# Gated linear attention into an expert layer: early low parts by TensorE and ScalarE, the forward scan in the gates' own tile, and a new order

## The chip, the cores and the metric

The kernel runs on one core of a Trainium2 chip. Time is device microseconds (us) of one execution, median of three. The engines are TensorE (PE; PEld is its weight load), VectorE (DVE), ScalarE (ACT), GpSimd (POOL) and SyncE (SP), which here only issues DMAs. Each engine works off its own list of instructions in the order of the program and waits on semaphores for the others.

## The reference

Two layers in float32. The first is a recurrence over 768 steps for each of 4 x 8 heads, with a 48 x 48 state; the second is an expert layer over all 3072 tokens:

```python
f = 1.0 / (1.0 + np.exp(-f_logit))
for t in range(S):                       # S = 768, B = 4, H = 8, D = 48
    state = f[:, :, t, :, None] * state + np.einsum('bhd,bhe->bhde', k[:, :, t], v[:, :, t])
    y[:, :, t] = np.einsum('bhd,bhde->bhe', q[:, :, t], state)
x = y.transpose(0, 2, 1, 3).reshape(B * S, H * D)      # 3072 x 384
h = x @ w_in                                           # 384 x 2048
return (h * np.clip(h + 3.0, 0.0, 6.0) / 6.0) @ w_out  # 2048 x 384
```

## The kernel before

**Units.** The recurrence is cut into 24 units: 6 chunks of 128 steps for each of 4 batches, all 8 heads at once; unit i is batch i % 4 of chunk i // 4. In a unit the gates go through a sigmoid on ACT (`gate`), and one DVE scan runs backwards over them (`back`, L320): products of the gates to the end of the chunk. They multiply k (`kmul`). The product over the whole chunk, limited below (`rend`, L336), is kept in `ends` and inverted (L337), and a second scan runs forwards from the inverse (`fwd`, L340, out into the tile `suffix` again); that multiplies q (`qmul`). TensorE then transposes k (`tk`, L404), forms scores (`att`, L385), the state's increment (`kv`, L423), and the output from the old state (`qs`, L454) and from the masked scores (`av`, L471). DVE masks (`mask`, L392); ACT or DVE carry the state on (`carry0`, `carry1`); `decay` multiplies the state by the chunk's product.

**Split numbers.** The large products run in fp32r, a faster format of TensorE that keeps fewer bits than float32. So each operand is split: a high part rounded to fp32r, and a low part, which is what is left. A product is three fp32r products: high x high, high x low, low x high. A unit's output y becomes a high part in `xts` by ACT (`xh`, L490) and a low part by DVE (`xl`, L493: y minus the high part); two DMAs (`hole`, L498) then fill rows between the heads.

**Conversion of the weights.** The 16 slices of weights (one per f, 128 columns of `w_in` and 128 rows of `w_out`) arrive as int64-packed float64 bits and are converted: loaded (`ld`), two pieces made by ACT (`z`, `cy`), the exponent's offset removed in 16-bit arithmetic on DVE (`mid`, `lim`, `dif`, `top`: L240, L246, L252, L256), the high part rounded by ACT (`high`, L261), the low part subtracted by DVE (`low` for a whole slice, or `lowi` and `lowo` for its halves: L264). For f = 0 to 7 the unrounded `w_out` slice is kept for a while (`wd`, a DMA).

**Expert layer.** Six groups of 512 tokens, 16 slices each. Token `mm1.n` (L517) is the first product of slice n % 16 of group n // 16: 9 fp32r instructions into one PSUM bank. ACT and DVE make the gate (`relu`, L527; `g`, L531), ACT the high part (`gh`, L536), DVE the low part (`gl`, L540), and `mm2.n` (L557) adds 9 fp32r instructions into three banks. In group 0, before its inputs are all there, slices 0 to 4 run as two halves of 256 tokens (`mm1a`, `mm1b`, L575), and slices 0 to 7 multiply by `w_out` in plain float32 (`mm2a`, `mm2b`, L593; `mm2x`, L565), which needs no `gh`, `gl` or `lowo`.

**Order.** Nothing is scheduled at run time. The table ORDER lists some 1360 tokens such as `mm1.35.4` (step, number, PSUM banks), written out ahead of time; each emits its instructions, and each engine keeps that order. `warm.n` are n products of zeros that keep TensorE's clock up. ON_POOL names the steps that run on GpSimd instead of DVE. Rings of buffers (`qkf` 3, `v` 3, `tg` 4, `gg` 3; `raw` 2, `w` 2, `y` 1) decide how far a step may run ahead.

Of the kernel before, what the change touches and what calls it, by code (L numbers as in the profile page):

```python
# [12 lines left out]
I16 = mybir.dt.int16  # L13
AF = mybir.ActivationFunctionType
# [25 lines left out]
qmul.0 qmul.1 kmul.3 decay.4 qmul.5 kmul.6 decay.6 kmul.7 decay.7 qmul.9 qmul.10 decay.10 qmul.11 decay.11 qmul.12  # L40
decay.12 qmul.13 decay.13 decay.14 kmul.15 qmul.15 kmul.16 decay.16 kmul.17 qmul.17 decay.17 qmul.18 decay.18 qmul.19
decay.19 qmul.20 decay.20 qmul.21 kmul.22 qmul.22 kmul.23 qmul.23 lowi.1 lowi.2 lowo.3 lowi.4 lowi.5 lowo.5 lowo.7
""".split()
ORDER = """
load.0 loadq.0 loadv.0 loadv.1 load.1 loadq.1 loadv.2 gate.0 ld.0 loadq.2 back.0 ld.1 rend.0 kmul.0 warm.16 tk.0.4
fwd.0 ktok.0 gate.1 qmul.0 load.2 warm.1 kv.0.0 carry0.0 back.1 att.0.2 carry1.0 qs.0.0 loadq.3 mask.0 rend.1 warm.2
av.0 kmul.1 xh.0 loadv.3 fwd.1 warm.1 tk.1.4 ktok.1 cy.0 xl.0 qmul.1 warm.1 kv.1.2 hole.0 z.0 load.3 att.1.0 carry0.1
mid.0 carry1.1 mask.1 warm.1 qs.1.2 lim.0 av.1 loadq.4 dif.0 xh.1 loadv.4 top.0 z.1 xl.1 gate.2 hole.1 cy.1 back.2
wd.0 ld.2 high.0 mid.1 kmul.2 rend.2 warm.12 tk.2.4 lowi.0 gate.3 fwd.2 ktok.2 warm.2 kv.2.0 lim.1 load.4 qmul.2
carry0.2 dif.1 att.2.2 carry1.2 back.3 ld.3 qs.2.0 mm1a.0.4 loadq.5 mask.2 kmul.3 rend.3 relua.0 av.2 ga.0 fwd.3  # L50
tk.3.2 xh.2 loadv.5 mm2a.0 ktok.3 z.2 xl.2 load.5 qmul.3 kv.3.2 gate.4 hole.2 top.1 att.3.0 carry0.3 carry1.3 mask.3
cy.2 wd.1 qs.3.2 loadq.6 back.4 av.3 high.1 loadv.6 xh.3 mid.2 kmul.4 xl.3 lowi.1 tk.4.4 mm1a.1.0 rend.4 hole.3 ktok.4
lim.2 fwd.4 gate.5 kv.4.2 relua.1 z.3 dif.2 ga.1 decay.4 ld.4 load.6 mm2a.1 top.2 back.5 cy.3 wd.2 mm1b.0.4 high.2
mid.3 kmul.5 mm1b.1.1 relub.0 lim.3 gb.0 lowi.2 tk.5.0 rend.5 relub.1 mm2b.0 carry0.4 ktok.5 dif.3 decay.5 ld.5
# [94 lines left out]
def gla_moe(ctx: ExitStack, tc: tile.TileContext, fg, qk, v, w, outT):  # L149
# [23 lines left out]
    weight = const.tile([128, NF, 2, WN], F32R, name="weight")  # L173
    win, wout = weight[:, :, :, :KT * 128], weight[:, :, :, KT * 128:]


# [645 lines left out]
```

## Time and profile before

| what | value |
|---|---|
| median of 3 runs | 513.59 us (512.88 to 513.95) |
| the profiled execution's own time | 512.78 us |
| its span, first to last instruction | 511.1 us |
| PE busy | 490.8 us (96%), 4960 instructions |
| DVE busy | 302.1 us (59%), 496 instructions |
| ACT busy | 207.1 us (41%), 331 instructions |
| POOL busy | 50.6 us (10%), 59 instructions |
| last product ends | 505.4 us; the rest is the last output |

Busy shares are means over the whole span. The prediction cuts the span into stages, and reads for each which engine never waits. The four parts of a row of the timeline are its start, its length, the engine and the instruction; idle time ahead of it and its releaser stand in brackets. In a row of grouped instructions the last part is idle time before them.

### The profile page before, as it was taken

Reading aid. Unit: us, or ns where it says so; the run is one execution under the profiler, and the core shown is the slowest. Engines: PE = TensorE matmul, PEld = TensorE weight load, DVE = VectorE, ACT = ScalarE, POOL = GpSimd, SP = SyncE. Lnnn points to the kernel's source line nnn. Section 1 sums busy time; section 2 is a strip of 40 time slices with the busy share of each in tenths; the row PEclk is TensorE's granted clock in tenths of the full one; section 3 lists DMA queues with packets and bytes.
Section 4 is the critical chain, followed back from the end, with each engine's and each line's share of the span. In section 5 each row is a group of like instructions: output and inputs, shape, how many; then the busy total and the mean of one; then the engine's idle time right before and its main releaser. Section 6 shows DMA issues by size and latency. Waiting matters only on the chain.

```text
span 511.1 us, 11476 instructions
## 1 busy us (share of the span) xinstructions
PE 490.8 (96%) x4960; PEld 388.7 (76%) x4960; DVE 302.1 (59%) x496; ACT 207.1 (41%) x331; POOL 50.6 (10%) x59
## 2 busy tenths in 40 slices
PE   8779999999999999999999999999999999999995
PEld 4468966777788888878887788887888788788874
DVE  5799999998955683364465524787433342333331
ACT  3556656764432253342242424244323341333231
POOL 2022422000211010020021000204000000000000
PEclk9899999999999999999999999999999999999999
DMA  8886666821302230330112200713300000200002
GB/s 279 260 246 194 216 200 233 256 94 41 99 19 79 62 99 0 109 96 16 52 28 81 62 0 2 191 56 106 87 0 1 8 1 0 63 1 1 0 1 67
DMA packets 25705, 43.53 MB, mean 85 GB/s; under 512 B 2608, under 2 KB 18224, under 8 KB 25648
## 3 DMA queue, kind: packets, MB, share of 16 engines
q1 hardware_dynamic: 25648, 42.73, 27.9%
q8 instruction: 41, 0.67, 0.5%
q14 instruction: 16, 0.13, 0.1%
HBM read 34.07 MB, written 4.72 MB: 76 GB/s over the span
## 4 chain that ended last, share of the span: by engine, by line
PE 51%; DMA 1%; DVE 1%; ACT 1%; issue 0%; POOL 0%; ACTq 0%
PE o L557 22%; PE pair L517 12%; PE single L517 11%; PE pair L608 3%; PE pair L454 1%; PE pair L471 1%; DMA qkf<-qk 1%; ACT tg L527 1%; PE pair L385 1%; DVE tg L531 1%; PE pair L423 1%; DMA outT<-os 1%; PE single L404 0%; PE pair L404 0%; DVE os L618 0%
## 5 line engine op out<-in xcount | busy, mean ns | idle before, releaser
L557 PE MATMUL o<-gg,weight 128*128 128x512 f32 x744 | 183.9, 398 | 0.6 <-ACT gg L536 0.6
L557 PEld LDWEIGHTS o<-gg,weight 128*128 128x128 f32 x744 | 138.2, 188 | 34.3 <-ACT gg L536 1.2
L517 PE MATMUL single<-xts,weight 128*128 128x512 f32 x423 | 108.2, 400 | 0.5 <-DVE tg L531 0.4
L517 PE MATMUL pair<-xts,weight 128*128 128x512 f32 x396 | 99.5, 396 | 0.6 <-DVE state L445 0.6
L540 DVE TENSOR_TENSOR gg<-tg,gg 128x512 fp32r<-128x512 f32 x88 | 60.6, 692 | 58.0 <-ACT gg L536 57.8
L517 PEld LDWEIGHTS single<-xts,weight 128*128 128x128 f32 x423 | 78.1, 188 | 20.4 <-DVE tg L531 1.2
L536 ACT ACTIVATE gg<-tg 128x512 fp32r<-128x512 f32 x88 | 55.4, 631 | 81.6 <-DVE tg L531 49.1
L517 PEld LDWEIGHTS pair<-xts,weight 128*128 128x128 f32 x396 | 73.5, 188 | 17.9 <-DVE state L445 1.0
L531 DVE SCALAR_TENSOR_TENSOR tg<-tg,single 128x512 f32<-128x512 f32 x47 | 32.1, 683 | 50.5 <-ACT tg L527 50.4
L527 ACT ACTIVATE tg<-single,half 128x512 f32<-128x512 f32 x47 | 32.3, 687 | 65.6 <-PE single L517 63.5
L531 DVE SCALAR_TENSOR_TENSOR tg<-tg,pair 128x512 f32<-128x512 f32 x44 | 30.0, 683 | 34.5 <-ACT tg L527 30.3
L527 ACT ACTIVATE tg<-pair,half 128x512 f32<-128x512 f32 x44 | 30.1, 687 | 35.3 <-PE pair L517 30.8
L490 ACT ACTIVATE xts<-pair 112x512 fp32r<-112x512 f32 x24 | 14.3, 595 | 53.8 <-PE pair L423 38.9
L320 DVE TENSOR_TENSOR_SCAN suffix<-gates,unit 112x516 f32<-112x516 f32 x24 | 30.2, 1261 | 6.7 <-ACT gates L314 6.4
L392 DVE TENSOR_TENSOR a<-pair,causal 128x512 f32<-128x512 f32 x24 | 16.4, 683 | 28.3 <-PE pair L471 26.1
L340 DVE TENSOR_TENSOR_SCAN suffix<-gates,rend 112x516 f32<-112x516 f32 x24 | 30.5, 1273 | 0.4 <-POOL qkf L333 0.2
L346 POOL TENSOR_TENSOR qkf<-qkf,suffix 112x512 f32<-112x512 f32 x16 | 21.5, 1345 | 88.1 <-DVE suffix L340 84.0
L349 POOL TENSOR_TENSOR decayed<-state,ends 112x192 f32<-112x192 f32 x13 | 7.0, 540 | 156.0 <-PE pair L454 123.5
L314 ACT ACTIVATE gates<-gates 112x512 f32<-112x512 f32 x24 | 15.0, 626 | 13.7 <-DMA gates<-fg 13.5
L493 DVE TENSOR_TENSOR xts<-pair,xts 112x512 fp32r<-112x512 f32 x24 | 16.4, 683 | 3.3 <-ACT xts L490 3.2
L385 PE MATMUL pair<-qkf 48*64 48x64 f32 x768 | 16.0, 220 | 2.4 <-issue 1.3
L423 PE MATMUL pair<-v,ktok 64*48 64x48 f32 (+1 forms) x768 | 15.9, 213 | 1.8 <-ACT ktok L411 1.0
(79 smaller groups left out, 420.7 us busy)
## 6 DMA issues: line engine op xcount, KB each, us to landing
raw<-w SPq DMA_DIRECT2D x16, 768.0 KB, 4.5
qkf<-qk SPq DMA_DIRECT2D x24, 448.0 KB, 4.4
gates<-fg SPq DMA_DIRECT2D x24, 226.2 KB, 3.0
v<-v SPq DMA_DIRECT2D x24, 200.0 KB, 4.3
outT<-os SPq DMA_DIRECT2D x17, 256.0 KB, 2.9
xts<-xts SPq DMA_DIRECT2D x48, 48.0 KB, 2.7
weight<-w SPq DMA_DIRECT2D x8, 192.0 KB, 3.3
outT<-os SPq DMA_DIRECT2D x2, 128.0 KB, 3.4
```

Source lines behind the costliest of these rows:

```text
L320: nc.vector.tensor_tensor_scan(flat(sf)[:, ::-1], gt[:, 1:][:, ::-1], flat(unit)[:, ::-1], 0.0, op0=ALU.mult, op1=ALU.add,)
L340: nc.vector.tensor_tensor_scan(flat(sf), gt[:, :NP * (C + 1)], flat(rend), 0.0, op0=ALU.mult, op1=ALU.add,)
L346: engine("qmul", i).tensor_tensor(parts_of(t, 0), parts_of(t, 0), split(sf[:, :, 1:]), op=ALU.mult)
L385: nc.tensor.matmul(d["at"][HC * odd:HC * (odd + 1), e, 2 * n + c], t[rs, 1, n, c, odd], t[rs, 0, n, c, odd], start=True, stop=True,)
L392: nc.vector.tensor_tensor(d["a"].rearrange("r p e t -> r e p t"), d["at"], causal.unsqueeze(1).unsqueeze(1).broadcast_to([128, 2, NP, HC]) ...
L423: nc.tensor.matmul(d["kv"][r:r + m, odd, c, n], d["ktok"][rs, 2 * n + part, r:r + m], heads_of(vt[rs], part, n, e)[:, :D], start=(odd, e) ...
L517: nc.tensor.matmul(h, win[:, f, a, k * 128:(k + 1) * 128], g["xt"][:, k, :g["n"] // C, b], start=i == 0, stop=i == 3 * KT - 1,)
L527: nc.scalar.activation(d["t"], d["h"], AF.Relu, bias=half, scale=1.0 / 6.0)
L531: nc.vector.scalar_tensor_tensor(d["t"], d["t"], 1.0, d["h"], op0=ALU.min, op1=ALU.mult)
L536: nc.scalar.activation(d["gg"][:, 0], d["t"], AF.Copy)
L540: engine("gl", f if g["name"] == "0" else NU).tensor_tensor(d["gg"][:, 1], d["t"], d["gg"][:, 0].bitcast(F32), op=ALU.subtract)
L557: nc.tensor.matmul(g["o"][m], wout[:, f, a, m * 128:(m + 1) * 128], g[f]["gg"][:, b], start=f == 0 and i == 0, stop=f == NF - 1 and i == 2 ...
```

## The change

Five things change, and the order of everything with them.

1. *Low parts of units 0 to 7.* A new constant, `minus`, is the negative of the identity, made by ACT at the start. A new step `ym` multiplies it with the high part of y and adds the product to y's PSUM bank, so that what is left there is the low part; `xl` is then a copy by ACT. Units 8 to 23 keep DVE's subtraction.
2. *Ends.* The limit from below (L336 before) is gone: the inverse is taken of the scan's own value, and ACT copies the value to `ends` (a new step `end`).
3. *Forward scan.* Its output overwrites the gates' tile instead of `suffix`. So `suffix` is free after `kmul`, `rend` and `end`, and the gates' tile is held until `qmul`.
4. *Conversion.* The 16-bit steps work on unsigned numbers with an offset; `lim` runs on ACT for f = 2, 4, 6, 8, 10, 12, 14 (ON_ACT) and ahead of `mid`. There are more tiles: `w` 3, `y` 2, and an own tile for `mid`, which before overwrote part of `raw`.
5. *Fewer float32 products.* Only slices 0, 1 and 2 run as halves with a float32 second product; slices 3 to 7 are full fp32r products. `wd`, `lowi` and `lowo` are there for f = 0, 1, 2 only; the rest uses `low`.

To make room, `tg` has 3 tiles and `gg` 2; the output's copies go through the `raw` ring; the last group keeps `gg` in tiles of `xts`. `warm` falls from 36 products to 27. ON_POOL is another list: 12 `kmul`, 13 `qmul`, 12 `decay`, `lowo.1`, `low.6`, `low.11`, `gl.9` (before 8, 16, 13, 4 `lowi` and 3 `lowo`).

```diff
+    minus = const.tile([PR, PR], F32R, name="minus")
+    nc.scalar.activation(minus, ident[:PR, :PR], AF.Copy, scale=-1.0)
...
-        {"qkf": 3, "v": 3, "ktok": 2, "tg": 4, "gg": 3, "a": 1},
+        {"qkf": 3, "v": 3, "ktok": 2, "tg": 3, "gg": 2, "a": 1},
...
-    cv = Ring(ctx.enter_context(tc.tile_pool(name="cv", bufs=1)), {"raw": 2, "w": 2, "y": 1})
+    cv = Ring(ctx.enter_context(tc.tile_pool(name="cv", bufs=1)), {"raw": 2, "w": 3, "y": 2, "t": 1})
...
     def conv_limit(f):
         y = conv[f]["y"]
-        nc.vector.tensor_scalar(
-            y, y, float(TOP_ONE - 32768), float(TOP_LAST), op0=ALU.max, op1=ALU.min
-        )
+        if on_scalar(f):
+            nc.scalar.activation(y, y, AF.Relu, bias=span, scale=-1.0)
+        else:
+            nc.vector.tensor_single_scalar(y, y, float(SPAN), op=ALU.min)
...
         def turn():
-            nc.vector.tensor_scalar_max(ends[:, i], sf[:, :, 0], END_LIMIT)
-            nc.vector.reciprocal(rend[:, :, 0], ends[:, i])
+            nc.vector.reciprocal(rend[:, :, 0], sf[:, :, 0])
+
+        def end():
+            nc.scalar.activation(ends[:, i], sf[:, :, 0], AF.Copy)
+
+        past = gt[:, :NP * (C + 1)]
 
         def forward():
-            nc.vector.tensor_tensor_scan(
-                flat(sf), gt[:, :NP * (C + 1)], flat(rend), 0.0, op0=ALU.mult, op1=ALU.add,
-            )
+            nc.vector.tensor_tensor_scan(past, past, flat(rend), 0.0, op0=ALU.mult, op1=ALU.add)
...
+        def ym():
+            for o in range(2):
+                nc.tensor.matmul(
+                    d["y"][:PR, o], minus, parts(0)[:, o], start=False, stop=True, skip_group_check=True,
+                )
+            d["less"] = True
+
         def xl():
-            nc.vector.tensor_tensor(parts(1), d["y"][:PR], parts(0).bitcast(F32), op=ALU.subtract)
+            if "less" in d:
+                nc.scalar.activation(parts(1), d["y"][:PR], AF.Copy)
+            else:
+                nc.vector.tensor_tensor(parts(1), d["y"][:PR], parts(0).bitcast(F32), op=ALU.subtract)
...
     def ghigh(g, f):
         d = g[f]
-        d["gg"] = sb.tile([128, 2, 512], F32R, tag="gg", name=f"gg{g['name']}_{f}")[:, :, :g["n"]]
+        if g["name"] == f"{NCB - 1}":
+            free = xts[:, f % KT].rearrange("p j b c -> p (j b c)")
+            d["gg"] = free.rearrange("p (b n) -> p b n", b=2)
+        else:
+            d["gg"] = sb.tile([128, 2, 512], F32R, tag="gg", name=f"gg{g['name']}_{f}")[:, :, :g["n"]]
```

What the table does is seen in the lists of the engines. The first place is DVE's list from unit 1's second scan on. Tiles are named by their role; `a` is the masked scores, `top` and `mid` (before `raw`) are conversion tiles, `gates`, `suffix` alternate by unit. Before:

```order
L340 SCALAR_TENSOR_TENSOR suffix_77<-gates_76,rend 112x516
L493 TENSOR_TENSOR xts<-pair_70,xts 112x2x2x128
L240 TENSOR_SCALAR raw_127<-top_252 128x768
L392 TENSOR_TENSOR a_305<-pair_70,causal 128x2x4x64
L246 TENSOR_SCALAR top_252<-top_252 128x768
L252 TENSOR_TENSOR top_252<-top_252,raw_127 128x768
L256 SCALAR_TENSOR_TENSOR w_283<-top_252,w_283 128x768
L493 TENSOR_TENSOR xts<-pair_71,xts 112x2x2x128
L320 SCALAR_TENSOR_TENSOR suffix_75<-gates_74,unit 112x516
```

and in the change:

```order
L367 SCALAR_TENSOR_TENSOR gates_76<-gates_76,rend 112x516
L372 TENSOR_TENSOR qkf_132<-qkf_132,gates_76 112x512
L343 SCALAR_TENSOR_TENSOR suffix_75<-gates_74,unit 112x516
L418 TENSOR_TENSOR a_305<-pair_71,causal 128x2x4x64
L359 RECIPROCAL rend<-suffix_75 112x4
L367 SCALAR_TENSOR_TENSOR gates_74<-gates_74,rend 112x516
L269 TENSOR_SCALAR mid_348<-top_339 128x768
L372 TENSOR_TENSOR qkf_137<-qkf_137,gates_74 112x512
L262 TENSOR_SCALAR top_339<-top_339 128x768
```

The subtractions into `xts` are gone from DVE, unit 1's q product has come to it from GpSimd, and unit 2's scans stand ahead of the first slice's conversion.

The second place is the start of ACT's list. Before:

```order
L196 ACT_TABLE_LOAD
L196 ACTIVATE table<-half 128x1
L314 ACTIVATE gates_74<-gates_74 112x4x128
L411 ACTIVATE ktok_158<-single 128x448
L314 ACTIVATE gates_76<-gates_76 112x4x128
```

and in the change:

```order
L198 ACT_TABLE_LOAD
L198 ACTIVATE minus<-ident 112x112
L213 ACT_TABLE_LOAD
L213 ACTIVATE table<-half 128x1
L337 ACTIVATE gates_74<-gates_74 112x4x128
L362 ACTIVATE ends<-suffix_75 112x4
```

A second load of function tables now stands ahead of unit 0's gates, since the copy that makes `minus` comes before the first sigmoid.

The third place is TensorE's list where group 0 gets going (`th` is the gate's half tile, `o` an output bank). Before:

```order
L593 MATMUL o_0_482<-th_1_620,weight 128x256
L593 MATMUL o_1_483<-th_1_620,weight 128x256
L593 MATMUL o_2_484<-th_1_620,weight 128x256
L575 MATMUL single<-xts,weight 128x256 x9
L575 MATMUL pair_70<-xts,weight 128x256 x9
L404 MATMUL pair_70<-ident,qkf_447 128x112 x4
```

and in the change:

```order
L633 MATMUL o_0_567<-th_2_619,weight 128x256
L633 MATMUL o_1_568<-th_2_619,weight 128x256
L633 MATMUL o_2_569<-th_2_619,weight 128x256
L615 MATMUL pair_71<-xts,weight 128x256 x18
L553 MATMUL pair_70<-xts,weight 128x512 x18
L430 MATMUL single<-ident,qkf_623 128x112 x4
```

Behind slice 2's halves the change goes on with the full products of slices 3 and 4, where the order before goes on with halves.

More of the change, by code (lines that the diff above doesn't have):

```diff
@@ L13 @@
 I16 = mybir.dt.int16
+U16 = mybir.dt.uint16
 AF = mybir.ActivationFunctionType
@@ L48 @@
[L48 to L52, printed above, removed]
@@ new lines @@
+relub.1 top.4 mm1.3.0 relub.2 back.5 loadq.6 high.4 z.5 low.4 mm1.4.1 load.6 end.5 cy.5 rend.5 kmul.5 gb.2 gb.0 ld.7
+gb.1 mid.5 tk.5.4 fwd.5 cy.6 mm2b.0 ktok.5 lim.5 lim.6 decay.5 mm2b.1 loadv.4 dif.5 relu.3 qmul.5 loadv.5 z.6 g.3
+att.4.2 lowo.1 mm2b.2 mask.4 gh.3 ld.8 relu.4 mid.6 gl.3 gate.6 mm2.3 top.5 z.7 loadv.6 dif.6 cy.7 g.4 kv.4.2 high.5
+ld.9 top.6 kv.5.0 gh.4 low.5 mm1.5.4 high.6 mid.7 gl.4 load.7 z.8 carry0.5 low.6 mm2.4 carry0.4 relu.5 carry1.5
+carry1.4 cy.8 g.5 gh.5 lim.7 ld.10 back.6 qs.4.0 lim.8 att.5.2 av.4 z.9 loadq.7 gl.5 mm1.6.4 dif.7 gate.7 mask.5
```

251 lines of the change are left out of this document (135 added, 116 removed).

## The prediction

> **What bounds the kernel now.** I read the busy time by stage first, then who waited for whom, then the timeline at the stage's ends. Columns of the first fence: stretch and its length, then busy time (instructions) of PE, PEld, DVE, ACT and POOL, granted clock, DMA share, GB/s.
>
> ```profile
> 26.04:112.87 86.83, 80.95 (x1130) 64.32 (x1121) 83.37 (x151) 58.35 (x88) 17.55 (x14) 1.00 0.65 206
> 130.00:505.39 375.39, 371.88 (x3367) 299.21 (x3366) 186.28 (x294) 128.37 (x207) 27.50 (x28) 1.00 0.16 46
> ...
> 4.54:39.12 34.58, 29.73 (x49) 0.95 0.89 269
> ```
>
> From 26 to 113 us DVE works 83.4 of 86.8 us: it sets the pace there. From 130 us to the last product TensorE works 371.9 of 375.4 us, so there only its own amount of work counts. The last row is DVE alone in the first stretch: 29.7 of 34.6 us, nearly 5 us lost to waits. So the end is fixed by how early TensorE gets from DVE all it needs for group 0. I take two points of the trace, `ga.1` (second float32 gate) and `gl.13` with `mm2.13`:
>
> ```profile
> 4.54 1.23 DVE L320 TENSOR_TENSOR_SCAN suffix<-gates,unit 112x516 f32<-112x516 f32 x1 [2.85 <-ACT gates L314]
> ...
> 38.71 0.41 DVE L588 SCALAR_TENSOR_TENSOR th<-th,pair 128x256 f32<-128x256 f32 x1
> 39.17 1.56 PE L593 MATMUL o<-th,weight 128*128 128x256 f32 x6 [1.09 <-DVE th L588]
> ...
> 112.18 0.69 DVE L540 TENSOR_TENSOR gg<-tg,gg 128x512 fp32r<-128x512 f32 x1
> 112.53 2.37 PE L557 MATMUL o<-gg,weight 128*128 128x512 f32 x9
> ```
>
> DVE starts at 4.54, ends `ga.1` at 39.12 and `gl.13` at 112.87; `mm2.13` starts at 112.53. Both orders have the same work left for TensorE at `mm2.13`: the change has done one `mm1` more (2.1) and unit 8 less (about 2.0). So its start compares them.
>
> **Part 1: DVE's list gets shorter.** Mean ns stand ahead of the last bar.
>
> ```profile
> L493 DVE TENSOR_TENSOR xts<-pair,xts 112x512 fp32r<-112x512 f32 x24 | 16.4, 683 | 3.3 <-ACT xts L490 3.2
> L336 DVE TENSOR_SCALAR ends<-suffix 112x4 f32<-112x4 f32 x24 | 10.5, 436 | 0.0
> L246 DVE TENSOR_SCALAR top<-top 128x768 int16<-128x768 int16 x16 | 5.5, 344 | 0.0
> L240 DVE TENSOR_SCALAR raw<-top 128x768 int16<-128x768 int16 x16 | 6.1, 382 | 1.4 <-ACT w L227 1.0
> L256 DVE SCALAR_TENSOR_TENSOR w<-top,w 128x768 int16<-128x768 int16 x16 | 16.5, 1029 | 0.0
> L340 DVE TENSOR_TENSOR_SCAN suffix<-gates,rend 112x516 f32<-112x516 f32 x24 | 30.5, 1273 | 0.4 <-POOL qkf L333 0.2
> L346 DVE TENSOR_TENSOR qkf<-qkf,suffix 112x512 f32<-112x512 f32 x8 | 5.5, 684 | 0.0
> L264 DVE TENSOR_TENSOR weight<-w,weight 128x768 fp32r<-128x768 f32 x8 | 7.6, 952 | 0.0
> L264 DVE TENSOR_TENSOR weight<-w,weight 128x384 fp32r<-128x384 f32 x4 | 2.2, 543 | 0.0
> L540 DVE TENSOR_TENSOR gg<-tg,gg 128x512 fp32r<-128x512 f32 x88 | 60.6, 692 | 58.0 <-ACT gg L536 57.8
> ```
>
> To `ga.1` the change lacks 4 `xl` (-2.7), 5 limits of `ends` (-2.2), one forward scan with its inverse (-1.5) and one `lim` (-0.3); it has two `qmul` from GpSimd (+1.4), two `lowi` (+1.1), one `top` (+1.0) and one `mid` (+0.4) more: -2.8. All of DVE's 48 instructions to `ga.1` come to 32.9 us by such means, in 34.6 us of time, a factor of 1.05; the change's come to 30.1. With the same factor `ga.1` ends at 4.5 + 31.6 = 36.1, **3.0 us earlier**. Bounds: with the factor of the whole list to `gl.13` (113.0 by means in 108.3 us, 0.96) 33.4, or 5.7 earlier; if ACT's longer list makes DVE wait for what it saves, nothing.
>
> From `ga.1` to `gl.13` the differences are 4 `xl` (-2.7), 4 limits (-1.7), 5 `lim` (-1.7), unit 8's scan, products and carries, which the change does later (about -3.5), a `top` (-1.0), and on the other side 4 `gl` and 2 `g` more for full products (+4.1) less 4 half gates (-1.7), and whole low parts in place of halves (+0.5, `lowi` and `lowo` together); with the small ones 80.1 goes to 71.6 by means. The stage's factor is 73.75 / 80.1 = 0.92, which gives 65.9 us for the change. The unsigned forms of `mid`, `lim` and `dif` are not in the trace; they have the sizes of the old ones and I price them alike. If each of the some 32 in this stage cost the 0.6 of `dif` instead of the 0.35 of `mid`, it would be 5 us, a bound.
>
> The 0.436 of the limit on `ends` is largely a wait:
>
> ```profile
> 27.39 1.19 POOL L333 TENSOR_TENSOR qkf<-qkf,suffix 112x512 f32<-112x512 f32 x1 [12.95 <-DVE suffix L320]
> 27.76 0.85 DVE L336 TENSOR_SCALAR ends<-suffix 112x4 f32<-112x4 f32 x1
> 28.64 0.18 DVE L337 RECIPROCAL rend<-ends 112x4 f32<-112x4 f32 x1
> ```
>
> It ends at 28.61, 0.03 after GpSimd's product. The Trainium skill (SBUF: State Buffer, Who interferes with whom) calls the port pair of DVE and GpSimd an exclusive lock, held for a whole instruction; by that rule the wait would pass to the next DVE instruction that needs the pair, and the rows agree as far as they go. By rows alone: an inverse of the same size with no wait takes 0.18 (third row), so some 0.26 of each limit is wait that may land on the instruction behind, 2.3 us over nine, in both spans; it is one more reason why I stay off the good ends.
>
> **Part 2: TensorE's list stays as long.** Prices come from starts in a row:
>
> ```profile
> 226.20 2.10 PE pair L517 x9
> 228.31 2.11 PE o L557 x9
> ...
> 40.38 1.42 PE L575 MATMUL single<-xts,weight 128*128 128x256 f32 x9
> 41.64 1.23 PE L575 MATMUL pair<-xts,weight 128*128 128x256 f32 x9
> 42.71 0.55 PE L404 MATMUL pair<-ident,qkf 112*128 112x112 f32 x4
> 43.09 1.47 PE L593 MATMUL o<-th,weight 128*128 128x256 f32 x6
> 44.22 1.42 PE L575 MATMUL single<-xts,weight 128*128 128x256 f32 x9
> ...
> 317.71 0.46 PE L454 MATMUL pair<-qkf,decayed 48*64 48x64 f32 x16
> 319.70 2.36 PE L557 MATMUL o<-gg,weight 128*128 128x512 f32 x9
> ```
>
> A full `mm1` or `mm2` takes 2.10, a half `mm1` 1.16 (the mean of 1.26 and 1.07), a half float32 `mm2` 1.13, a transposition 0.38, the rest of a unit 1.99. A slice in halves with float32 is 4.58 and in full 4.20, so slices 3 and 4 save 0.8; slices 5 to 7, whose float32 `mm2` at two halves' price is 2.26, save 0.2 each. A `ym` is two instructions of 256 columns: 0.25 at the rate of L575, and 0.75 at L593's; it is fp32r as L575 is, so 0.25, 2.0 for eight. Altogether about 0.7 more. From `ga.1` to `mm2.13` the change's list is 12 `mm1` and 10 `mm2` (46.2), 3 half `mm1` (3.5), 5 half `mm2` (5.7), units 4 to 7 (9.1) and 4 `ym` (1.0): 65.5 us.
>
> So after `ga.1` TensorE needs 65.5 and DVE 65.9, where now TensorE takes 73.4 (39.17 to 112.53), paced by DVE. Two full engines that hand work to each other through in-order lists do not both run without a wait; one full engine loses none to the other today. I take half of the 7.5 us that would be won: **3.8**, bounds 0 and 7.5.
>
> **Part 3: what is added elsewhere.** ACT's nearest rows to the new work are these:
>
> ```profile
> L490 ACT ACTIVATE xts<-pair 112x512 fp32r<-112x512 f32 x24 | 14.3, 595 | 53.8 <-PE pair L423 38.9
> L236 ACT ACTIVATE top<-raw 128x768 int16<-128x768 int16 x16 | 14.5, 907 | 3.9 <-DVE w L256 3.8
> ```
>
> ACT gets, up to `gh.13`, 7 `xl` (0.6 as L490), 7 `lim` (0.9 as L236), 8 `end` (under 0.3 each, as the smallest) and 5 more `gh` (0.6), less 4 half gates; it worked 58.4 of 86.8 us, so some 14 us more fit, but its waits now reach DVE: `mid.2` stands behind `lim.2` and `low.f` behind `high.f`. This is what halved the gain above.
>
> Moving `hole.7` is what comes late next. In the change `ym.7`, `xl.7` and two DMAs stand between `av.7` and `mm1.16`, and only `mm2.13` and `mm1.15` (4.2) run meanwhile:
>
> ```profile
> xts<-xts SPq DMA_DIRECT2D x48, 48.0 KB, 2.7
> 122.60 1.21 SPq L498 DMA_DIRECT2D xts<-xts  x2
> ```
>
> 0.25 + 0.6 + 0.6 for the first issue + 2.7 after the second is 4.2 to 4.8: **0.4 lost** (0 to 2). On SP the load of a later unit's gates now waits for `qmul` instead of `fwd`; behind it stand slice loads, but each has its landing (4.5) before ACT reaches it, so I count nothing; without that cover it is one `qmul`, 0.7. The outputs' copies find the `raw` ring empty, as its last slice is converted before them. The nine `warm` that go only filled waits; if the clock, 0.95 on average to 39 us, were at 0.5 while slices 0 to 2 start, it costs 1.2 for each half `mm1` there.
>
> The rings `gg` 2 and `tg` 3 matter in rows of `mm2`:
>
> ```profile
> 302.91 14.87 PE L557 MATMUL o<-gg,weight 128*128 128x512 f32 x63
> 305.21 0.63 ACT L536 ACTIVATE gg<-tg 128x512 fp32r<-128x512 f32 x1 [7.65 <-PE o L557]
> 305.88 0.69 DVE L540 TENSOR_TENSOR gg<-tg,gg 128x512 fp32r<-128x512 f32 x1 [7.59 <-ACT gg L536]
> ```
>
> A freed buffer's high part is ready 0.8 us after the product's end (305.01), its low part 1.6. With two buffers the next but one product wants the first after 2.1 and the second, which only its last three instructions read, after 3.5. That holds with 1.3 to spare; I take **0.5 lost** over the 80 products, for the few where a scan of 1.3 comes between.
>
> The second table load stands in a gap:
>
> ```profile
> 0.82 1.28 ACT L196 ACT_TABLE_LOAD   x1 [0.82 <-PEq L812]
> 2.26 0.20 ACT L196 ACTIVATE table<-half 128x1 f32<-128x1 f32 x1 [0.16 <-POOL half L194]
> 3.87 0.63 ACT L314 ACTIVATE gates<-gates 112x512 f32<-112x512 f32 x1 [1.41 <-DMA gates<-fg]
> ```
>
> ACT idles 1.41 before the first gates; `minus` (0.2) and a load (1.28) take 1.5 of that, so the gates start some 0.1 late: nothing. The Trainium skill (ScalarE: Activation LUTs, What ACT_TABLE_LOAD costs) gives 1283 ns for the load, which the row agrees with, and a drain of about 1380 ns on top for every switch of sets. The row shows no drain, as the next instruction starts 0.16 later, but that load is the first and nothing is switched.
>
> **The sum.** 3.0 + 3.8 - 0.4 - 0.5 = 5.9 us. The profiled execution took 512.78 (span 511.1 and 1.7 around it) and would take 506.9; the median of the runs lies 0.8 above it, so the forecast is **507.7**. Everything taken at its good end gives 5.7 + 7.5 - 0 = 13.2, or 500.4.
>
> **Rivals.**
>
> *Both engines keep pace.* Stage gain 7.5, start 3.0 to 5.7: 501 to 504. For it: DVE's idle time in its stage is only 3.5 us. Against it: ACT's fuller list. Chance 0.15.
>
> *A drain at the table switch.* If the second load holds ACT 1.4 us longer (as the page on ScalarE has it), everything behind the first gates moves by 1.4: 509.1. For it: nothing in the trace; against it the 0.16. Chance 0.12.
>
> *ACT takes DVE's place.* If each slice in conversion waits 0.5 on ACT more (`high` and `cy` behind `xl` and `lim`), 14 slices take 7 us and nothing is left: 512.5 to 514.5. For it: ACT's work in the stage goes from 58 to some 70 of 80 us. Chance 0.11.
>
> *Two `gg` buffers are too few.* Place: `mm2` of groups 1 to 5. If TensorE waits 0.07 per product on average over 80, the 5.9 are gone; at 0.15 the run is 514 and slower, at 0.3 it is 526. It decides if ACT or DVE is late by more than the spare 1.3 in one of five products. For it: DVE's scans of 1.3 stand in the same list; against it: DVE is half idle then (186 of 375). Chance 0.12.
>
> **How the numbers follow.** Forecast 0.50, with 505 to 510.5 as its own range; the rivals 0.15, 0.12, 0.11, 0.12. A change of 0.2%, 1 us, is about what a measurement of this kernel can tell. Faster is the forecast, the first two rivals and some of the third: 0.78; within 0.2% 0.10 (third and the start of the fourth); slower 0.12. The range goes from 502.5, in the first rival, to 514.5, which takes in the third and the mild part of the fourth.
>
> **What would show it.** DVE's `ga.1` (a 128x256 gate) ending near 36 us and `mm2.13` starting near 106; busy DVE in that stage still above 90%, with ACT above 80%. `ym` near 0.12 an instruction, the unsigned steps 0.35 to 0.6. From 130 us on a busy TensorE above 98%, with no growing waits on `gg`. I am wrong if TensorE waits for ACT from 40 to 110 us, if waits on `gg` come to several us after 130, or if `ga.1` is not earlier.

## The result: slower by 0.8%, not faster by 1.2%

The changed kernel takes 517.4 us in the median (514.7 to 523.1), the kernel before, timed beside it, 513.9 (511.8 to 516.4). The ratio is 1.0076, with a 95% interval of 1.0055 to 1.0096; it is taken from fast runs alone, without the 523.1, and is not the quotient of the medians. The forecast was 507.7, its range ended at 514.5. The profiled execution took 517.08, with a span of 515.3.

Of the profile's page after the change, span and busy time:

```profile
span 515.3 us, 11464 instructions
PE 491.2 (95%) x4952; PEld 390.5 (76%) x4952; DVE 297.2 (58%) x458; ACT 224.6 (44%) x375; POOL 53.4 (10%) x58
```

The moves between engines came as planned: DVE lost 4.9 us, ACT took 17.5, TensorE has the same work. The loss is idle time of TensorE: span less busy time is 20.3 us before and 24.1 after. Busy time by stage says where. The stages end at the first `mm2` behind `ga.1` and at `mm2.13`; columns as in the prediction (stretch, its length, busy time of PE, PEld, DVE, ACT, POOL with the number of instructions, granted clock, DMA share, GB/s). Before:

```profile
0.00:39.17 39.17, 30.39 (x624) 19.21 (x624) 30.45 (x52) 19.85 (x36) 7.52 (x20) 0.96 0.85 257
39.17:112.53 73.36, 71.08 (x863) 56.23 (x863) 69.97 (x129) 50.12 (x74) 14.56 (x11) 1.00 0.63 202
112.53:511.10 398.57, 389.35 (x3480) 313.23 (x3474) 201.64 (x317) 137.16 (x222) 28.50 (x28) 1.00 0.17 47
```

After:

```profile
0.00:39.37 39.37, 31.32 (x601) 21.09 (x601) 28.02 (x46) 25.22 (x49) 3.98 (x19) 0.91 0.79 230
39.37:110.84 71.47, 69.16 (x787) 56.01 (x788) 67.98 (x110) 58.86 (x88) 16.97 (x10) 1.00 0.64 205
110.84:515.30 404.46, 390.73 (x3567) 313.38 (x3565) 201.20 (x304) 140.55 (x240) 32.44 (x29) 1.00 0.17 47
```

- **To `ga.1`:** no gain, 39.4 for 39.2, where 3.0 was forecast, although DVE has 2.4 us less to do.
- **`ga.1` to `mm2.13`:** 1.9 us shorter, where 3.8 was forecast. TensorE idles for 2.3 us here in both kernels. What the stage won is what TensorE's own list lost, 71.1 to 69.2.
- **Behind `mm2.13`:** 5.9 us longer, where 0.9 was forecast. TensorE has 1.4 us more busy time and 4.5 more idle time.

The timeline shows the waits of TensorE behind `mm2.13`. After, from 111 to 345 us, all rows with idle time ahead:

```profile
141.60 2.36 PE L553 MATMUL pair<-xts,weight 128*128 128x512 f32 x9 [0.63 <-ACT ktok L437]
174.15 2.35 PE L553 MATMUL pair<-xts,weight 128*128 128x512 f32 x9 [0.65 <-DVE state L471]
180.21 2.36 PE L553 MATMUL single<-xts,weight 128*128 128x512 f32 x9 [1.21 <-ACT ktok L437]
196.23 0.60 PE L430 MATMUL single<-ident,qkf 112*128 112x112 f32 x4 [0.86 <-POOL qkf L356]
208.09 0.46 PE L480 MATMUL pair<-qkf,decayed 48*64 48x64 f32 x16 [0.47 <-DVE state L471]
286.31 2.33 PE L553 MATMUL single<-xts,weight 128*128 128x512 f32 x9 [1.01 <-DMA xts<-xts]
296.03 2.36 PE L553 MATMUL single<-xts,weight 128*128 128x512 f32 x9 [0.73 <-ACT ktok L437]
298.65 2.36 PE L553 MATMUL pair<-xts,weight 128*128 128x512 f32 x9 [0.25 <-DVE tg L567]
331.40 2.36 PE L553 MATMUL single<-xts,weight 128*128 128x512 f32 x9 [0.48 <-DVE tg L567]
```

Before, in the same stretch:

```profile
135.14 2.36 PE L517 MATMUL pair<-xts,weight 128*128 128x512 f32 x9 [0.60 <-DVE state L445]
220.16 0.24 PE L423 MATMUL pair<-v,ktok 64*48 64x48 f32 x2 [0.73 <-issue]
225.62 0.58 PE L404 MATMUL pair<-ident,qkf 112*128 112x112 f32 x4 [0.44 <-POOL qkf L346]
277.56 2.36 PE L517 MATMUL single<-xts,weight 128*128 128x512 f32 x9 [0.38 <-DVE tg L531]
```

Nine waits and 6.3 us against four and 2.2. A product of nine that follows a wait also costs a little more: the next instruction starts 2.19 behind it (174.15 to 176.34), where it is 2.10 in a row. The 2.36 in these rows is no price, since it reaches past the start of the next instruction; a row without a wait ahead can be as long (186.43, 2.37). None of the waits is for `gg`. Most are for units 8 to 18: their keys, states, low parts. The chain of waits, from 160 us, gives a reason (start, length, what):

```profile
160.06 4.29 DMA qkf<-qk
...
164.60 1.59 POOL qkf L372
166.19 0.02 issue
166.20 3.58 DMA gates<-fg
...
169.87 0.64 ACT gates L337
...
170.59 1.23 DVE suffix L343
171.82 1.54 DVE qkf L356
173.37 0.09 DVE rend L359
173.46 0.25 DVE middle L464
```

The loads of q and k for unit 11 land, GpSimd multiplies q, and only then the load of unit 13's gates is issued (166.20), because the in-place scan keeps the tile until `qmul`. The prediction had priced that at nothing. This is theory 1: **the hold of the gates tile**. Theory 2: **the order of the late units** makes the waits, whatever holds a tile. Theory 3: the **short rings** of `tg` and `gg` make them.

### The profile page after: what moved, and what is told of

Same layout as the page of the kernel before. It is cut to its first block, busy times and chain, and to the rows that moved or that the text cites. A ratio compares the mean times of both kernels' runs of the same rounds, so it can differ in the third digit from the quotient of the medians.

```text
span 515.3 us, 11464 instructions
## 1 busy us (share of the span) xinstructions
PE 491.2 (95%) x4952; PEld 390.5 (76%) x4952; DVE 297.2 (58%) x458; ACT 224.6 (44%) x375; POOL 53.4 (10%) x58
## 4 chain that ended last, share of the span: by engine, by line
PE 81%; DMA 6%; DVE 5%; ACT 4%; issue 2%; POOL 1%; SPq 0%; ACTq 0%; POOLq 0%; DVEq 0%
PE o L597 32%; PE pair L553 20%; PE single L553 16%; DMA gates<-fg 3%; PE pair L648 2%; DMA xts<-xts 2%; PE pair L480 2%; PE pair L411 2%; PE pair L497 2%; PE pair L449 1%; ACT tg L563 1%; DVE tg L567 1%; DVE suffix L343 1%; PE o L633 1%; PE single L430 1%
## 5 line engine op out<-in xcount | busy, mean ns | idle before, releaser
L597 PE MATMUL o<-gg,weight 128*128 128x512 f32 x693 | 170.4, 398 | 0.0
L597 PEld LDWEIGHTS o<-gg,weight 128*128 128x128 f32 x693 | 128.5, 188 | 30.5
L553 PE MATMUL pair<-xts,weight 128*128 128x512 f32 x468 | 117.3, 397 | 1.5 <-DVE state L471 0.7
L553 PEld LDWEIGHTS pair<-xts,weight 128*128 128x128 f32 x468 | 86.7, 188 | 22.1 <-DVE state L471 1.1
L553 PE MATMUL single<-xts,weight 128*128 128x512 f32 x369 | 94.2, 399 | 3.4 <-ACT ktok L437 1.9
L553 PEld LDWEIGHTS single<-xts,weight 128*128 128x128 f32 x369 | 67.8, 188 | 20.9 <-ACT ktok L437 2.8
L367 DVE TENSOR_TENSOR_SCAN gates<-gates,rend 112x516 f32<-112x516 f32 x24 | 30.5, 1272 | 0.7
L372 POOL TENSOR_TENSOR qkf<-qkf,gates 112x512 f32<-112x512 f32 x13 | 17.6, 1354 | 111.1 <-PE pair L449 64.4
L597 PE MATMUL o<-xts,weight 128*128 128x512 f32 x96 | 25.3, 397 | 0.1
L597 PEld LDWEIGHTS o<-xts,weight 128*128 128x128 f32 x96 | 17.8, 188 | 4.9 <-ACT xts L576 0.5
```

Of the source, the lines that this page charges most:

```text
L367: nc.vector.tensor_tensor_scan(past, past, flat(rend), 0.0, op0=ALU.mult, op1=ALU.add)
L372: engine("qmul", i).tensor_tensor(parts_of(t, 0), parts_of(t, 0), split(to), op=ALU.mult)
L553: nc.tensor.matmul(h, win(f, a, k), g["xt"][:, k, :g["n"] // C, b], start=i == 0, stop=i == 3 * KT - 1,)
L597: nc.tensor.matmul(g["o"][m], wout(f, a, m), g[f]["gg"][:, b], start=f == 0 and i == 0, stop=f == NF - 1 and i == 2, skip_group_check=True,)
```

## Experiments

In the tables the ratio is to the kernel before, timed in the same round, with its 95% interval; then the start of `mm2.13` and what follows to the end of the span, from one profile each. The start of `mm2.13` scatters: it lies between 108.1 and 113.5 in seven profiles with the same program up to there. What follows it hardly depends on that: in five profiles with the changed late part it is 404.2 to 404.7 at starts from 108.3 to 111.3, in a sixth 406.3.

### A third tile for the gates

The 2 KB for it came from `mid`, which went back into the `raw` tile.

```diff
-    for i in range(2):
+    for i in range(3):
         gates.append(const.tile([PR, FW], F32, name=f"gates{i}"))
...
-        t = conv[f]["t"] = cv.tile([128, WN], U16, tag="t", name=f"mid{f}")
+        t = conv[f]["t"] = conv[f]["raw"].bitcast(U16)[:, 2 * WN:3 * WN]
```

> The changed kernel with a third tile for the gates (unit i uses tile i modulo 3), so that a load no longer waits until the product with q of the unit two before has read the in-place scan. The 2 KB for it come from the middle part of the conversion, which goes back into the raw tile as in the kernel before. Theory 1 (the in-place forward scan holds the gates tile, and loads, gates, scans and with them the attention units come late): load 2 issues near 5 us instead of 9.64, the loss of 5 us more than before between 111 and 300 us shrinks by at least half, the time falls from 517.4 to 511-515. Theory 2 (the new order of the late units costs, whatever the tiles): load 2 earlier, but the time within 1 us of 517.4. Theory 3 (two gg and three tg buffers): within 1 us of 517.4 as well.

The second kernel is the same with two gates tiles.

> Control for the run with three gates tiles: the changed kernel with two gates tiles, and only the middle part of the conversion back in the raw tile. All theories: within 1 us of 517.4; if a raw tile held until the subtraction delays the next slice's load, up to 3 us more, all of it before 111 us.

| run | median | ratio |
|---|---|---|
| three gates tiles, `mid` in `raw` | 544.3 | 1.0579 (1.0533 to 1.0625) |
| two gates tiles, `mid` in `raw` | 546.0 | 1.0628 (1.0578 to 1.0678) |

Both miss their expectation by far, and so say nothing on the theories. `raw` is now held until `dif`, and SP, where loads of units stand behind those of slices, waited 69.6 us for it in the second run. The own tile for `mid` is no small part of the change: in this order its absence costs some 28 us.

### The hold of the gates tile

The late units' gates can live in the conversion's three `w` tiles, which are idle by then.

```diff
         def load():
+            if i >= 10:
+                held["gt"] = cv.tile([128, WN], F32, tag="w", name=f"late{i}")[:PR, :FW]
-            nc.sync.dma_start(out=gt, in_=fg[u])
+            nc.sync.dma_start(out=held["gt"], in_=fg[u])
```

> The changed kernel, but the gates of units 10 to 23 live in the three w tiles of the conversion, which are idle by then; so a late load waits for the unit three before and not two before. Nothing else is changed, and nothing ahead of 111 us. Theory 1 (the hold of the gates tile by the in-place scan delays the late units): the stretch behind mm2.13 shrinks from 404.5 by 2 to 5 us, the time is 512.5 to 515.5. Theory 2 (the order of the late units costs by itself): the loads issue earlier, but the time stays within 1 us of 517.4.

The same for unit 2 alone (`if i == 2`), for the start:

> The changed kernel, but the gates of unit 2 live in a w tile, so that the loads of the units 2, 3 and 4 no longer wait for a product with q; the first slice's load, which stands behind that of unit 2 on SP, moves up with it. Nothing behind that is changed. Theory 1 (the hold also costs at the start): load 2 issues near 5 us instead of 9.64, back.2 starts by 14.5 instead of 15.56, ga.1 ends by 38.3 instead of 39.31, the time falls by 1 to 2 us. Rival (the start is set by the order on DVE and ACT and by TensorE's half clock): ga.1 within 0.4 us of 39.31 and the time within 1 us of 517.4.

Both, and `loadq.0` ahead of `loadv.0` and `loadv.1`:

> Both moves of the gates (unit 2 and units 10 to 23 in w tiles) in the changed kernel, and the first load of q and k issued ahead of the first two of v, as in the kernel before. Theory 1: 510 to 513.5, below the kernel before. Theory 2 with the start's rival: within 1.5 us of 517.4.

And the reverse, the scan in place in the kernel before:

```diff
             nc.vector.tensor_tensor_scan(
-                flat(sf), gt[:, :NP * (C + 1)], flat(rend), 0.0, op0=ALU.mult, op1=ALU.add,
+                gt[:, :NP * (C + 1)], gt[:, :NP * (C + 1)], flat(rend), 0.0, op0=ALU.mult, op1=ALU.add,
             )
```

> The kernel before with one edit: the forward scan writes over the gates, and the product with q reads it there; order, buffers and everything else as before. Theory 1: slower than before by 2 to 6 us (516 to 520 against 513.9), with loads that wait for the product with q. Theory 2 and theory 3: within 1 us of the kernel before.

In that run 14 loads still stood ahead of the product with q of the unit two before. So those products took other numbers, and waited for that load; its 531.3 us (ratio 1.0336) are not the price of the hold. The next run has the loads moved.

> The kernel before with the forward scan written over the gates and read there by the product with q, and with 14 loads of gates (units 4 to 6, 8, 10, 12 to 14, 16 to 20, 22) put behind the product with q of the unit two before, as they must be then. Theory 1: slower than before by 2 to 6 us. Theory 2: within 1 us of the kernel before.

| run | median | ratio | `mm2.13` | rest |
|---|---|---|---|---|
| the change | 517.4 | 1.0076 (1.0055 to 1.0096) | 110.8 | 404.5 |
| late gates in `w` tiles | 516.7 | 1.0076 (1.0049 to 1.0102) | 109.5 | 404.7 |
| gates of unit 2 in a `w` tile | 517.4 | 1.0112 (1.0079 to 1.0145) | 109.2 | 404.4 |
| both, `loadq.0` first | 516.6 | 1.0077 (1.0046 to 1.0107) | 108.6 | 406.3 |
| before, scan in place | 521.4 | 1.0188 (1.0156 to 1.0220) | 114.0 | 403.4 |

In the order before, the hold costs 8.5 us, above what theory 1 expected. That includes the 14 loads, which it forces to a later place. In the changed order its removal wins nothing: load 13 issues at 163.2 for 166.2, with a `mm2.13` that is 1.3 earlier, and the waits behind stay. It now stands right behind a `hole` in SP's list, whose two DMAs are issued from 161.84 to 163.15. Theory 1 falls as the cause of the late loss in this order. With both moves the profile starts `mm2.13` 2.2 earlier and loses 1.8 of it behind (rest 406.3); there TensorE waits 2.2 us for GpSimd's `kmul.15`.

### Local repairs of the late order

`ktok.12` ahead of `mm1.28`, `ktok.18` ahead of `gh.49`, three `kmul` from GpSimd to DVE:

```diff
-tk.12.4 gl.26 gate.14 mm1.28.1 relu.27 back.14 ktok.12 g.27
+tk.12.4 gl.26 gate.14 ktok.12 mm1.28.1 relu.27 back.14 g.27
```

> The changed kernel with five local moves in its late order and nothing else: ktok.12 ahead of mm1.28 and relu.27, ktok.18 ahead of gh.49, and kmul.13, kmul.14 and kmul.15 on DVE instead of GpSimd (kmul.15 behind g.30). Theory 2 (the order of the late units costs by itself): the waits of mm1.29 and mm1.52 on ktok (1.2 and 0.7) and of tk.14 on GpSimd's kmul (0.9) go, each with the 0.26 that the first product after a wait takes longer; the stretch behind mm2.13 shrinks from 404.5 by 2 to 4 us and the time is 513.4 to 515.4. Theory 1 (the hold of the gates tile): what is gained at these places is lost at the next ones, within 1 us of 517.4.

> The same five moves on top of both moves of the gates and of the earlier load of q and k. Theory 2: its wait of 2.2 for GpSimd's kmul.15 and those on ktok (1.2 and 1.0) go, time 511 to 514, 2.5 to 5.5 below the run without the five moves (516.6). Theory 1 has no further gain here: within 1 us of the run with the five moves alone. Rival (something not seen yet gives it back): 515.5 to 517.

> As the run before it, with 14 tiny products (16 columns, into the idle bank) behind the 19 warm ones. TensorE's stall in att.1 that no engine explains (1.3 to 1.9) comes in both kernels after the 220th product of the program (in before after 16+4+1+48+32+16+2+32+1+4+1+48+15 products, in the changed kernel after 19+4+32+48+1+16+32+4+2+48+14). If it hangs on that count, it now falls ahead of att.1, where TensorE waits for its bank anyway, att.1 ends about 1 us earlier, and the time falls by 0.5 to 1.5 us against the run without them. If it hangs on att.1 or on the moment, it stays where it was and the time is the same.

| run | median | ratio | `mm2.13` | rest |
|---|---|---|---|---|
| five moves | 515.9 | 1.0064 (1.0036 to 1.0092) | 111.3 | 404.4 |
| five moves, both gates moves, `loadq.0` | 516.3 | 1.0043 (1.0021 to 1.0066) | 108.3 | 404.2 |
| the same with 14 tiny products | 514.2 | 1.0015 (0.9993 to 1.0036) | 110.4 | 403.4 |

The first run lands between the two theories' expectations, the second in that of its rival. With the five moves alone the waits of `mm1.29` and `mm1.52` are gone (the 0.26 that the expectation adds to each wait is 0.09 by starts). But `tk.14` still waits 0.8, now for DVE, `tk.15` 1.0, and `mm1.53` comes 3.6 us after `mm1.52` instead of 2.6. The rest stays at 404. So these five slips are not the late loss: where their waits went, others came. On the tiny products: the stall in `att.1` moved from behind its 14th product to behind its second (the count of 220 would put it ahead of the first), but ended at the same moment, 16.3 us, so the move hides nothing. Why this kernel is some 0.3% faster than the one without them (the intervals overlap) stays open.

### Which of the late parts costs

All of these have the program of the change up to `mm2.13`. First, with its tiles and rings, and the late order of the kernel before; high parts (`gh`) come later where two `gg` buffers ask for it.

> The changed kernel's steps, tiles and rings, and its order up to the product of slice 13 of group 0 (110.84 us in its profile); from there the order of the kernel before, with the placing on GpSimd of its late units, and with steps put later only where the two gg and three tg buffers ask for it. Theory 2 (the late order costs): the stretch behind that product takes some 399 to 400 us instead of 404.5, the time is 512 to 514. Theory 1 (the hold of the gates tile costs in either order): 515 to 518. Theory 3 (the short rings cost): 515 to 520, with waits on gg or tg in the rows of the products.

Then the late part of the kernel before as a whole: order, forward scan into `suffix`, four `tg` and three `gg` buffers, for which the freed conversion tiles give the room.

```diff
+            to = flat(sf) if i >= 8 else past
-            nc.vector.tensor_tensor_scan(past, past, flat(rend), 0.0, op0=ALU.mult, op1=ALU.add)
+            nc.vector.tensor_tensor_scan(to, past, flat(rend), 0.0, op0=ALU.mult, op1=ALU.add)
...
+        elif n % 4 < 3:
+            d["t"] = cv.tile([128, WN], F32, tag="w", name=name)[:, :g["n"]]
```

> The changed kernel up to mm2.13 of group 0, and behind it all three late parts as in the kernel before: its order, its forward scan into suffix (units 8 to 23, with the limit on ends), and four tg and three gg buffers (made from the conversion's w tiles and from the freed tg tiles). If the late loss of the changed kernel (404.5 from the start of mm2.13 against 398.6 in before) is made behind that point and by these three together, the stretch returns to 398 to 400 and the time is 510 to 513. If the early part leaves something behind that costs later, 515 to 518.

> As the run before it, with one of the three put back as in the changed kernel: the forward scan of units 8 to 23 in place, the ends copied by ACT, and nine loads of gates put behind the product with q of the unit two before, as they must be then. If the hold of the gates tile costs in this order as it did in the kernel before, 4 to 8 us longer than the run before it; if it costs only at the start, within 1 us of it.

> As the first of these runs, with the rings back at three tg and two gg buffers, so that eleven high parts (gh) and what hangs on them come later in the list. By the rival of the two gg buffers: TensorE waits for ACT's gg in this stretch, 3 to 12 us longer than the first run, with those waits in its rows; if the rings are long enough, within 1 us.

> As the first of these runs, with the gates of unit 2 in a w tile and the first load of q and k ahead of those of v. In an order that is not tied to the start later on, the earlier start should now reach the end: mm2.13 1 us earlier on average, the time 0.5 to 1.5 us below the first run. If what is gained at the start is lost before mm2.13, the same as the first run.

| late part behind `mm2.13` | median | ratio | rest |
|---|---|---|---|
| the change (its order, in place, short rings) | 517.4 | 1.0076 (1.0055 to 1.0096) | 404.5 |
| order before, scan into `suffix`, long rings | 513.8 | 1.0013 (0.9988 to 1.0037) | 400.1 |
| order before, in place, long rings | 519.4 | 1.0124 (1.0099 to 1.0149) | 406.7 |
| order before, scan into `suffix`, short rings | 527.0 | 1.0284 (1.0255 to 1.0313) | 415.9 |
| order before, in place, short rings | 534.5 | 1.0403 (1.0370 to 1.0435) | 422.7 |
| second row, start moves | 513.2 | 0.9981 (0.9957 to 1.0005) | 400.3 |

So the late loss is made in the late part. With the late part of before, 4.4 of the 5.9 us behind `mm2.13` are back and 1.5 stay open; the median, 0.8 above what was expected, is 3.6 below the change's. In that order the hold costs 5.7 us, the short rings 13.3, both 20.7 (20 by the ratios, as that run belongs to another round). Each price takes in the steps that must stand later in the list for it. TensorE's longest waits say so, with the hold and long rings (111 us to the end):

```profile
PE o L625 <- ACT gg L604: 3.5, 1, 3.5
PE single L562 <- ACT ktok L446: 1.0, 1, 1.0
```

The first of these is the hold. The load of a unit's gates is issued when the product with q of the unit two before has ended (234.87, on DVE). ACT, which has that `gate` ahead of a `relu` and a `gh` in its list, waits for the load, and TensorE for `gh`:

```profile
234.90 0.32 SPq L333 DMA_DIRECT2D gates<-fg  x1
237.63 0.63 ACT L346 ACTIVATE gates<-gates 112x512 f32<-112x512 f32 x1 [4.08 <-DMA gates<-fg]
240.87 3.91 PE L625 MATMUL o<-gg,weight 128*128 128x512 f32 x9 [3.49 <-ACT gg L604]
```

And with the short rings:

```profile
PE o L601 <- ACT gg L580: 4.4, 6, 0.8
PE single L557 <- DVE tg L571: 3.1, 2, 2.9
PE pair L484 <- DVE state L475: 2.5, 2, 1.5
```

With both, the changed order pays 3.6 us instead of 20.7, and pays in waits that name neither `gg` nor the gates' loads. That relieving the hold there gave nothing fits a list that is made around both and has no step that would use a freed tile; this is argued, not shown. The changed order with long rings was not run, nor with long rings and the free tile. So how the 3.6 divide between the order itself, the hold and the rings stays open. The start moves win 0.6, within the noise.

### Who sets the pace before `mm2.13`

The low parts alone, in the kernel before: `ym` on TensorE and a copy on ACT for units 0 to 7.

```diff
         def xl():
-            nc.vector.tensor_tensor(parts(1), d["y"][:PR], parts(0).bitcast(F32), op=ALU.subtract)
+            nc.scalar.activation(parts(1), d["y"][:PR], AF.Copy)
```

> The kernel before with one part of the change alone: the low parts of units 0 to 7 by ym on TensorE and a copy on ACT in place of the subtraction on DVE; order, tiles and rings as before, ym placed between xh and xl. By the prediction's own steps DVE's list, which paces the stretch from ga.1 to mm2.13, gets 5.4 us shorter (eight times 0.68), TensorE's 2 us longer (eight times 0.25), so mm2.13 starts 2 to 4 us earlier than 112.53 and the time is 510 to 512. Rival (xl waits in ACT's in-order list, behind w copies and relus, and hole and mm1 come late): within 1 us of the kernel before.

Here `ym` of the units 4 and 5 stands behind another unit's `kv` in the same bank, so the low parts of these two come out otherwise than the reference's; kinds, sizes and waits are those of the step.

With the start moves and the late part of before (513.2 above), `lim` back on DVE, or `ym` away and `xl` back on DVE:

```diff
-lim.2 lim.4 lim.6 lim.8 lim.10 lim.12 lim.14
```

> As the run with the start and the late order changed (513.19), with the seven limits of the even slices on DVE instead of ACT (mid and dif of these slices in the form of the odd ones). DVE gets some 2.5 us more, ACT some 6 less. If TensorE's own list sets the stretch from ga.1 to mm2.13 (69.2 busy of 71.5 in the changed kernel, 71.1 of 73.4 in before), the stretch stays within 1 us and the time within 1 us of 513.2. If DVE sets its pace, as the prediction had it, the stretch and the time get 2 to 3 us longer.

> As the same run, without ym: the low parts of units 0 to 7 are subtracted by DVE as in the kernel before. TensorE's list gets 1.7 us shorter (eight pairs at 0.22), DVE's 5.4 longer. If TensorE's own list sets the stretch from ga.1 to mm2.13, it stays or gets up to 1 us shorter, and the time is 511.5 to 513.5. If DVE sets its pace, the stretch gets 2 to 3 us longer (four of the eight subtractions lie in it) and the time is 515 to 519.

| run | median | ratio | stage `ga.1` to `mm2.13` | PE busy in it | DVE busy in the span |
|---|---|---|---|---|---|
| before | 513.4 | 1 | 73.4 | 71.1 | 302.1 |
| before, low parts by `ym` | 513.2 | 1.0000 (0.9983 to 1.0016) | 75.2 | 71.9 | - |
| start moves, late part of before | 513.2 | 0.9981 (0.9957 to 1.0005) | 73.4 | 70.6 | 297.9 |
| and `lim` on DVE | 512.1 | 0.9965 (0.9938 to 0.9992) | 72.8 | 69.7 | 300.3 |
| and no `ym` | 512.6 | 0.9987 (0.9965 to 1.0010) | 71.8 | 68.6 | 301.7 |

In the second row DVE is busy for less of the stage (67.7 of 75.2 us), and idles for more. Its busy times in the stage:

```profile
38.88:114.07 75.19, 71.89 (x871) 56.80 (x871) 67.72 (x125) 52.54 (x79) 14.63 (x11) 1.00 0.61 198
```

Its waits there (whom DVE waited for, us in total, times, longest):

```profile
DVE raw L242 <- ACT top L238: 2.2, 3, 1.1
DVE th L600 <- ACT th L596: 2.2, 4, 1.5
```

In the kernel before, the first is not among the waits of this stage and the second is 0.7: what DVE no longer does, it waits for on ACT. And putting work back on DVE does not make the kernel slower: 512.1 and 512.6 for 513.2, where DVE as the bound would have given 515 or more. So DVE does not set the pace of this stage. In each row TensorE's idle time is 2.3 to 3.3 us, so it is nearly full throughout. That its list alone sets the pace is not shown: without `ym` it is 2 us shorter in this stage and DVE's list longer, and the time falls by 0.6, within the noise. The lengths of the stage in the table can't decide it, as they are 71.3 to 74.3 in the seven profiles of one early program. The kernel with `lim` on DVE is the only one that is faster than before beyond its interval, by 0.35% in the ratio and 0.24% in the medians.

## Why the prediction was wrong

The sum was 5.9 us faster; the profiles are 4.2 slower. Of the 10.1 between them 3.2 lie ahead of `ga.1`, 1.9 between `ga.1` and `mm2.13`, and 5.0 behind.

**"There only its own amount of work counts"**, said of TensorE from 130 us on, failed by the most. That it hardly waits held for the order before with its long rings and its gates tile free early. Without the free tile the same order takes 5.7 us more, with short rings 13.3. The step read a property of one order and its buffers as one of the stage.

**"DVE sets the pace" from 26 to 113 us** is the step that failed first in time. The row gave DVE 83.4 of 86.8 us and TensorE 81.0, and I took the fuller one. Cut at `ga.1`, where the start's waits end, TensorE is busy for 71.1 of 73.4 us and DVE for 70.0. Both were full, so 2.3 us of TensorE's idle time were there to be won by faster supply, not 7.5.

**"After `ga.1` TensorE needs 65.5"** was a price too low: its busy time is 69.2. I had priced every product by starts in a row. By starts in this stage the 12 `mm1` and 10 `mm2` take 47.7 for 46.2 (mostly 2.19 where a small product stands ahead or behind), the five half `mm2` 7.1 for 5.7 with one short wait, the units' small products 10.7 for 9.1 (a stall of 1.6 left out). So the 3.8 was half of a gain that was mostly not there; the 1.9 that came is the shorter list, in one profile of a stage that scatters by 3.

**Part 1, `ga.1` 3.0 earlier,** failed in its factor. DVE's list is shorter by 2.4 (2.8 forecast), but to `ga.1` DVE idles 7.5 us instead of 4.9. Three of its waits, and one of TensorE, which stands behind the second of them:

```profile
15.56 1.23 DVE L343 TENSOR_TENSOR_SCAN suffix<-gates,unit 112x516 f32<-112x516 f32 x1 [1.18 <-ACT gates L337]
18.98 0.69 DVE L418 TENSOR_TENSOR a<-pair,causal 128x512 f32<-128x512 f32 x1 [2.19 <-PE pair L411]
26.61 0.69 DVE L418 TENSOR_TENSOR a<-pair,causal 128x512 f32<-128x512 f32 x1 [0.99 <-PE pair L411]
...
18.37 0.50 PE L411 MATMUL pair<-qkf 48*64 48x64 f32 x18 [1.85 <-issue]
```

A factor from one list does not carry to another: a wait for TensorE or a DMA does not shrink with DVE's work. Over the seven profiles with this start `ga.1` ends between 36.7 and 39.8, 38.5 on average, so the gain is 0.6 against before's one profile. Part of the first wait looks like the hold again, as load 2 issues at 9.64, behind `qmul.0`. But with its own tile the load issues 5.1 earlier and takes longer, so that it lands only 0.8 earlier (start, length). In the change:

```profile
9.64 5.17 DMA gates<-fg
```

and with the own tile:

```profile
4.58 9.39 DMA late<-fg
```

`ga.1` came at 38.2 with this tile, and with `loadq.0` first at 36.5, both within the scatter or just below it. And in the change the chain that ended last runs through ACT without a pause from 29.86 to 36.77, with two `xl` and a `lim` in it, 2.0 us that the change moved there.

**The nine fewer `warm`, "nothing":** from 19 to 24 us the granted clock (third number from the end) is 0.52. After:

```profile
19.00:24.00 5.00, 4.38 (x86) 2.97 (x83) 4.20 (x8) 2.81 (x5) 0.00 (x0) 0.52 0.97 359
```

Before:

```profile
19.00:24.00 5.00, 4.43 (x18) 1.74 (x16) 4.20 (x9) 4.18 (x7) 0.00 (x0) 0.84 0.73 210
```

In this stretch the kernel before does 12 `warm`, the changed one `av.1`, `tk.2`, three `warm` and `kv.2` (1.52 for 0.91). In every profile with the changed start the clock here is between 0.50 and 0.82; in the three other profiles of the order before (scan in place twice, `ym`) it is 1.00 twice and 0.65 once. That the fewer `warm` make it is possible, and was not tried alone. The Trainium skill (TensorE: Matmul & The Clock Gate, Part 1: The HAM clock gate) has the clock at half after an idle window of about 3.4 us and at full after as long a time of sustained work. These rows do not decide it: in the 5 us ahead of this stretch TensorE is busy for 2.25, and its longest idle time there is 1.85.

**The gates' load behind `qmul`, "nothing" or "0.7":** 5.7 and 8.5 in two orders. I had counted one `qmul`; but the load stands in SP's list ahead of `loadq`, `loadv` and `hole`, each unit's chain starts from it, and ACT's list has other work behind its `gate`.

**The rings, "0.5":** no wait on `gg` came, as forecast, and the rival of the two `gg` buffers did not happen in its own form. But it is the nearest to what did: the rings cost 13.3 in the order before, and 3.6 in the changed order together with the hold and that order itself, in other rows.

**What was right.** The second table load costs nothing: it starts at 2.43, `table` at 3.72, `gate.0` at 3.83 (3.87 before). So that rival is out: no drain shows in these rows. The 1380 ns that the Trainium skill (ScalarE: Activation LUTs, What ACT_TABLE_LOAD costs) gives for it are not seen in this case. `ym` takes 0.24 a pair, the unsigned steps 0.35 to 0.42 (`mid`, `lim`), ACT is busy for 82% of the stage, DVE for 95%. DVE idles for 3.5 us of it, 3.4 before, so the rival in which DVE waits for ACT did not come in this stage; it is the kernel before with `ym` that shows such waits. `mm1.16` does not wait for `hole.7`; the 0.4 was not lost.

## What to carry to other kernels

Where two engines are both above 95% in a stage, look at the one whose list the change does not shorten: its idle time is the most that can be won. A tile that is held longer or a ring that is one shorter need not show a wait of its own, as in the changed order here; try it alone in an order that has it free. A mean factor of waiting, taken from one list, did not hold for the next.

## What had not been expected of the hardware

TensorE stalls once for 0.4 to 2.3 us at 14 to 19 us, with no engine to wait for, after its 220th product in the kernel before, in the change, and in the kernel before with `ym`. With 14 products put ahead the stall began 12 products earlier in the step and ended at the same time. A second one, 1.3 to 2.0 us, comes at `kv.7` near 91 us in each profile with this early program. That it is the supply of instructions fits both, and was not shown.

Profiles of one early program differ by 5.4 us at `mm2.13`, with granted clocks of 0.50 to 0.66 from 19 to 24 us and, in one of them, 0.92 from 90 to 111 (1.00 in the others). So a gain of 1 or 2 us at the start cannot be read from one profile.
